# Moving the first query products between the passes of other units, and GpSimd's first sum behind VectorE's denominators, in a kernel of linear attention beside a dense SiLU layer

## The chip, the cores and the metric

The kernel runs on one core of one Trainium2 chip. The metric is device time in microseconds (us) of one execution; the median of three executions of the kernel before is 152.88 us, and they lie between 152.51 and 153.01 us. The profiled execution is one more, with a time of its own.

The engines are called PE (TensorE's matmuls), PEld (TensorE's weight loads, which run beside matmuls), DVE (VectorE), ACT (ScalarE), POOL (GpSimd) and SP (which issues transfers). PSUM has eight banks, numbered 0 to 7; a tile that is written by PE and read by DVE or ACT takes a pair of neighbouring banks, and the pair is named by its first bank.

## The reference, cut to what matters

```python
def _A_ref(x, wqkv, w_phi, wo):          # S=2048 rows, D=448, H=16 heads, Dh=28
    q, k, v = split(x @ wqkv)
    pq, pk = q @ w_phi, k @ w_phi        # per head
    phi_q = concat([softmax(pq), softmax(-pq)])
    phi_k = concat([softmax(pk), softmax(-pk)])
    kv = einsum("bhsf,bhsd->bhfd", phi_k, v)
    z  = einsum("bhsf->bhf", phi_k)
    num = einsum("bhqf,bhfd->bhqd", phi_q, kv)
    den = einsum("bhqf,bhf->bhq", phi_q, z)[..., None] + 1e-6
    return (num / den) @ wo              # heads laid side by side
def _B_ref(x, w1, w2):                   # w1: 448 x 1792, w2: 1792 x 448
    return silu(x @ w1) @ w2
xn = _layernorm(x)
return x + _A_ref(xn, ...) + _B_ref(xn, ...)
```

## The kernel before, in words

**Work and tiles.** The 2048 rows are 16 tiles of 128, taken as eight pairs (pair 0 to pair 7). After the layer norm each pair is transposed on PE (`xnT_tr` in `ln_tr`, L634: seven operations of two transposes each into a pair of banks, copied to `xnT` by DVE or ACT).

**Units and passes.** The first dense layer (`x @ w1`, then SiLU on ACT) is computed in units (`ffn1_chunk`, L743): two blocks of 128 hidden features for two pairs of rows, into one pair of banks. A contraction over 448 features is done in half arrays of 64 rows: an operation (`mms`, L445) issues two matmuls side by side, one on the upper and one on the lower 64 rows of the array, each into its own bank. `contract` (L476) makes a unit of two **passes**: a first of eight operations and a second of six, in which the two halves of the array change banks. Since the second pass adds to banks that the other half has written, its first operation waits on a semaphore until the last operation of the first pass has ended (`syncs`). Something put between the two passes on PE fills that wait. PE executes strictly in the order in which it was given its instructions.

**Order.** Every instruction is recorded in a list with its dependences, and a list scheduler (`schedule`, L218) puts the list of each engine in order. Where the order matters it is laid down by hand: `odeps` are edges within one engine that only order, `deps` are edges that become semaphore waits, and `chain` (L1012 to L1239) is the order of groups on PE from the key stage on.

**Stages.** (1) Layer norm, transposes and first units; (2) units for pairs 2 to 5, with the folding of `w_phi` into the weights of q and k; at its end the transposes of pairs 6 and 7 and the units of pairs 4 and 5 for blocks 8 to 11; (3) keys, values, exponentials (`k_macro`, `q_group`, `k_acc`); (4) the last units (blocks 12 and 13 for pairs 4, 5 and all 14 blocks for pairs 6, 7; called u[0] to u[7], each of two passes u[i][0], u[i][1]), the sum over the keys turned into the matrix `KVZ`, and between them the **query products** of pairs 0 and 1; (5) for each pair the second dense layer and `wo` (`out_pair`, L1186), with the query products of the pair after next.

**Query products and division.** `q_products` (L1082) makes for one tile of a pair eight operations of two matmuls of 60 columns; a pair's tile 0 goes to banks 2 and 3, its tile 1 to banks 4 and 5, for every pair. `uu[0]`, `uu[1]` are the two tiles of pair 0, `uu[2]`, `uu[3]` those of pair 1. `q_divide` (L1097) empties the banks on DVE, for pair 0 tile by tile: `R2` (L1108, reciprocals of the sums, from PSUM), `Dd` (L1110, one input from PSUM and one from SBUF), `den` (L1112, two inputs in SBUF), `rden` (L1115, one input in SBUF), `Gq` (L1116, `R2` times `rden`, two inputs in SBUF), `o12` (L1123, one input from PSUM and one from SBUF, which reads the banks out). The next products into these banks wait for that `o12`. Then POOL adds the two halves (`oadd`, L1145, both inputs in SBUF): for pair 0 first tile 0 (448 columns), then tile 1 in four pieces (8, 56, 336, 48 columns). The sums are transposed on PE (`oT_tr`), and the second layer's products read them.

Of the kernel before, what the change touches and what calls it, by code (L numbers as in the profile page):

```python
# [332 lines left out]
def bass_parallel_sum__linear_kernel_hedgehog__dense_activation_silu__prompt_kernel(  # L333
# [11 lines left out]
    NT, NPAIR = S // 128, S // 256  # L345
# [10 lines left out]
    with es:  # L356
        def sb(name, shape, dt):
            return es.enter_context(nc.sbuf_tensor(name, shape, dt))
# [48 lines left out]
        den = sb("den", [128, 2, 32], F32)  # L407
# [14 lines left out]
        P = _Prog()  # L422
# [8 lines left out]
        def d_dve(n, mode=1):  # L431
            return n * 1.042 / mode + 150.0
# [24 lines left out]
        def trs(parts, name):  # L457

            def fn(e):
                for dst, src, r in parts:  # L460
                    out = e.transpose(dst, src, ident[r, 64:128] if r == LO else ident[r, 0:64])  # L461
                return out
            P.op("pe", 32.0, fn, reads=[p[1] for p in parts] + [ident[:]], writes=[p[0] for p in parts],
                 table=64, name=name)

        def act(dst, src, func, name, table=None, scale=1.0):
            return P.op("act", d_act(_cols(src)), lambda e: e.activation(dst, src, func, scale=scale),  # L467
                        reads=[src], writes=[dst], table=table, name=name)

        def copy_dve(dst, src, name, dur):  # L470
            return P.op("dve", dur, lambda e: e.tensor_copy(dst, src), reads=[src], writes=[dst], name=name)  # L471
# [143 lines left out]
        def ln_stats(t):  # L615
            bnst(t)
            bnag(t)

        def ln_rstd(t0, t1):
            m2, r2 = mv[:, t0:t1, 1], rstd[:, t0:t1]  # L620
            v2, nh = ve[:, t0:t1], neghalf[:, t0:t1]
            P.op("dve", 160, lambda e: e.tensor_scalar(v2, m2, EPS_LN, None, ALU.add), reads=[m2], writes=[v2], name="ve")  # L622
            P.op("pool", 580, lambda e: e.tensor_tensor(r2, v2, nh, ALU.pow), reads=[v2, nh], writes=[r2], name="rstd")  # L623

        def ln_norm(p, t, eng="dve"):
            sl = p % NXN
            for c0, c1, o0 in (((0, D, 0),) if t % 2 == 0 else ((384, D, D), (0, 384, 512))):
                xn = xn_sb[:, sl, o0:o0 + c1 - c0]
                dur = 120 + (c1 - c0) * 0.6 if eng == "dve" else 120 + (c1 - c0) * 1.0
                P.op(eng, dur, lambda e, xn=xn, c0=c0, c1=c1: e.tensor_scalar(  # L630
                    xn, x_sb[:, t, c0:c1], mv[:, t, 0:1], rstd[:, t:t + 1], ALU.subtract, ALU.mult),
                    reads=[x_sb[:, t, c0:c1], mv[:, t, 0:1], rstd[:, t:t + 1]], writes=[xn], name="xn")

        def ln_tr(p, js, b0, eng):  # L634
            for i, j in enumerate(js):
                trs([(bank16[b0 + h][:, 64 * i:64 * i + 64], xn_sb[r, p % NXN, 128 * j:128 * j + 128], r)
                     for h, r in enumerate((UP, LO))], "xnT_tr")
            n = len(js)
            src = psum16[:, b0 * 1024:(b0 + 2) * 1024].rearrange("p (b c) -> p b c", b=2)[:, :, 0:64 * n].rearrange(
                "p b (j u) -> p b j u", u=64)  # L640
            dst = xnT[:, js[0]:js[-1] + 1, p, :].rearrange("p j (b u) -> p b j u", b=2)
            if eng == "act":
                act(dst, src, ACTF.Identity, "xnT_ev")
            else:
                copy_dve(dst, src, "xnT_ev", d_dve(128 * n, 2))
# [79 lines left out]
        def ln_pair(p, one_by_one=False):  # L725
            t0, t1 = 2 * p, 2 * p + 1
            for t in (t0, t1):
                ln_stats(t)
                if one_by_one:
                    ln_rstd(t, t + 1)  # L730
            if not one_by_one:
                ln_rstd(t0, t1 + 1)
            ln_norm(p, t0)
            ln_norm(p, t1)
            ln_tr(p, [0, 1, 2, 3, 4, 5, 6], {3: 4, NPAIR - 1: 2}.get(p, 6), "act" if p in LN_ACT else "dve")

        LN_ACT = (2,)
        silus = []
# [2 lines left out]
        units_done = []  # L741
# [100 lines left out]
        for p in range(2):  # L842
            for f0, f1, i0, i1 in ((0, 6, 0, 2), (0, 6, 2, 3), (6, 10, 0, 2), (10, FT, 0, 2)):
                if p == 1 and i0 == 0 and f0 < 10:
                    k = len(P.ops)
                    ln_pair(2 + f0 // 6, f0 > 0)
                    evp.append(P.ops[-1])
                    ln_late.append(P.ops[k:])
                    for o in P.ops[k:]:
                        if o.eng == "dve":  # L850
                            o.odeps.add(last1)
                passes.append(ffn1_single(p, f0, f1, i0, i1, next(banks_), f0 + p + i0 == 0))
                if p + f0 + i0 == 0:
                    k = len(P.ops)
                    evp.append(lnz_second(1))
                    for o in P.ops[k:]:
                        if o.eng == "dve":
                            o.odeps.add(ev0.id)
                    last1 = [o.id for o in P.ops if o.eng == "dve"][-1]
# [4 lines left out]
        turn = d2[:5] + d3[:6] + d2[5:] + d3[6:]  # L864
# [6 lines left out]
        for a, c in zip(order0, order0[1:]):  # L871
            for o in c:
                o.odeps.add(a[-1].id)
        k = len(P.ops)
        ln_pair(4)
        later4 = [o for o in P.ops[k:] if o.eng == "dve"]
        tr4 = [o for o in P.ops[k:] if o.name == "xnT_tr"]
        evp.append(P.ops[-1])
        unit_no[0] = 0
        ffn1_chunk(2, 2, 0, 4, (4, 0, 2))  # L880
        k = len(P.ops)
        ln_pair(5)
        later5 = [o for o in P.ops[k:] if o.eng == "dve"]
        for o in later4 + later5:
# [23 lines left out]
        for o in P.ops[k:]:  # L908
            if o.eng == "dve":
                o.odeps.add([a for a in later5 if a.name == "xn"][-1].id)  # L910

        def proj(p, W, b0, name):
            return contract([(lambda r, b: xnT[r, b, p, :], W,
                       [banks[b0 + par][:, 0:D] for par in range(2)], True, False)], D, True, True, name)
# [29 lines left out]
        def k_acc(p):  # L944

            sl, ops = p % NEK, []
            for t in range(2):
                first, last = p == 0 and t == 0, p == NPAIR - 1 and t == 1
                E3 = Ek[sl][:, t, :].rearrange("p (s c) -> p s c", s=2)
                for c in range(4):  # L950
                    parts = []
                    for i in range(4):
                        h = 4 * c + i
                        parts.append((banks[4][VW * i:VW * i + VW, 56 * c:56 * c + 56].rearrange("p (s f) -> p s f", s=2),
                                      vaug[sl][:, t, h, :], E3[:, :, h * DH:h * DH + DH], first and c == 0, last))
                    ops.append(mms(parts, "kv_mm", 50.0, 32))
            return ops
# [54 lines left out]
        chain = []  # L1012
# [22 lines left out]
        kv = k_acc(NPAIR - 3) + k_acc(NPAIR - 2) + k_acc(NPAIR - 1)  # L1035
# [38 lines left out]
        kv_tr = kv_transpose()  # L1074
# [20 lines left out]
        oadd_last = {}  # L1095
# [129 lines left out]
        u = units_done[k:]  # L1225
        uu = []
        for p in range(2):
            uu += marked(q_products, p)
            q_divide(p)
        uu = [uu[8 * i:8 * i + 8] for i in range(4)]  # L1230
        chain += [u[0][0], u[1][0], u[0][1], u[2][0], u[1][1], u[2][1], kv, u[3][0], kv_tr, u[3][1], u[4][0][:4], uu[0],
                  u[4][0][4:], uu[1], u[4][1], u[5][0], u[5][1], u[6][0], uu[2], u[6][1], u[7][0], uu[3], u[7][1]]
        for p in range(NPAIR - 1):
            out_pair(p)
        out_last(NPAIR - 1)
        chain = [c for c in chain + out_order if c]
# [20 lines left out]
        for e in ("pe", "act", "dve", "pool"):  # L1257
            cnt = 0
            for oid in order[e]:
                o = ops[oid]  # L1260
# [4 lines left out]
        for e in ENGINES:  # L1265
            for oid in order[e]:
                o = ops[oid]
# [88 lines left out]
```

## Time and profile before

| | |
|---|---|
| median of three executions | 152.88 us (152.51 to 153.01) |
| the profiled execution | 152.47 us |
| its span, first to last instruction | 150.8 us (1.67 us lie outside) |
| PE busy | 147.0 us, 2698 matmuls |
| DVE busy | 99.5 us |
| ACT busy | 73.0 us |
| POOL busy | 56.3 us |
| granted TensorE clock | 1.000 |

A line of the timeline gives the start, the time to the end of the last of a run of like instructions, the engine, the source line, the operation, the tiles, the count and, in brackets, the idle time ahead of it and what ended it. A matmul's shown duration includes its way through the array, so that neighbours overlap; the rate at which PE works is read from the starts. Units stand there as `psum<-xnT,w_sb`, query products as `psum<-KVZ,EqT`, the second dense layer as `psum<-w_sb,hT`, transposes of rows as `psum<-ident,xn_sb`. Two matmuls are one operation.

### The profile page before, as it was taken

The page shows a single profiled execution, that of the slowest core. Times are in us where ns is not written, and L with a number is a line of the kernel's source. Part 1 is how long each engine was busy: PE and PEld are TensorE (multiplying, and loading weights), DVE is VectorE, ACT ScalarE, POOL GpSimd, SP SyncE. Part 2 cuts the span into 40 slices and gives each one's busy share as a digit, 9 for nine tenths or more (in the row PEclk, how much of TensorE's full clock was granted, in tenths as well). Part 3 has the DMA queues.
Part 4 walks back from the last instruction along what each step waited for, and adds up shares of the span by engine and source line. Part 5 has one row for each costly group of instructions (what it writes and reads, how often), then busy time and mean ns, then how long its engine had stood idle before and what let it go on. Part 6 is the DMA issues. An engine that isn't in the chain of part 4 may idle for free.

```text
span 150.8 us, 5942 instructions
## 1 busy us (share of the span) xinstructions
PE 147.0 (98%) x2698; PEld 102.4 (68%) x2698; DVE 99.5 (66%) x189; ACT 73.0 (48%) x84; POOL 56.3 (37%) x85
## 2 busy tenths in 40 slices
PE   7999999999999999999999999999999999999992
PEld 6789988888844445446488885666666666665672
DVE  1989798965518999489693678748383939392203
ACT  3648865567699886888497555202020202022000
POOL 7135031020101788847993054370707070614000
DMA  4988374000004332253201000010101010101012
GB/s 119 347 257 262 99 218 130 5 4 4 4 0 122 126 122 67 55 151 49 36 12 16 4 0 4 4 61 4 61 4 61 7 61 4 61 0 65 0 65 61
DMA packets 9427, 10.30 MB, mean 68 GB/s; under 512 B 1626, under 2 KB 9018, under 8 KB 9402
## 3 DMA queue, kind: packets, MB, share of 16 engines
q1 hardware_dynamic: 8938, 9.65, 21.8%
q8 instruction: 21, 0.34, 0.9%
q10 hardware_dynamic: 464, 0.28, 0.6%
q14 instruction: 4, 0.03, 0.1%
HBM read 7.37 MB, written 1.84 MB: 61 GB/s over the span
## 4 chain that ended last, share of the span: by engine, by line
PE 98%; DVE 0%; issue 0%
PE psum L448 94%; PE psum L461 3%; DVE out_raw L1174 0%; PE psum L1059 0%
## 5 line engine op out<-in xcount | busy, mean ns | idle before, releaser
L448 PE MATMUL psum<-w_sb,hT 64*128 64x448 bf16 (+2 forms) x504 | 46.8, 328 | 0.0
L448 PE MATMUL psum<-xnT,w_sb 64*128 64x256 bf16 (+1 forms) x768 | 46.5, 268 | 0.1
L448 PEld LDWEIGHTS psum<-xnT,w_sb 64*128 64x128 bf16 x768 | 36.1, 94 | 4.2 <-PE psum L448 0.3
L467 ACT ACTIVATE hT<-psum 128x1024 bf16<-128x1024 f32 (+1 forms) x29 | 28.2, 993 | 13.7 <-PE psum L448 13.7
L448 PEld LDWEIGHTS psum<-w_sb,hT 64*128 64x128 bf16 x504 | 25.0, 94 | 14.3
L1145 POOL TENSOR_TENSOR xn_sb<-wraw 128x448 bf16<-128x448 f32 (+4 forms) x39 | 20.7, 562 | 36.2 <-DVE wraw L1123 31.6
L467 ACT ACTIVATE oT<-psum 128x896 bf16<-128x896 bf16 x8 | 7.3, 917 | 40.2 <-PE psum L461 40.2
L939 POOL TENSOR_TENSOR scr<-scr,Rk 128x1792 bf16<-128x1792 bf16 (+2 forms) x7 | 19.0, 2725 | 13.6 <-ACT scr L467 11.1
L1123 DVE TENSOR_TENSOR wraw<-psum,Gq 128x1792 f32<-128x1792 f32 (+1 forms) x10 | 16.4, 1650 | 0.8
L1174 DVE TENSOR_TENSOR out_raw<-psum,x_sb 128x896 bf16<-128x896 f32 (+2 forms) x9 | 8.8, 980 | 9.6 <-PE psum L448 9.4
L467 ACT ACTIVATE EqT<-psum 128x1024 bf16<-128x1024 f32 x14 | 13.6, 1021 | 3.1 <-PE psum L448 3.1
L1108 DVE RECIPROCAL R<-psum 128x64 f32<-128x64 f32 (+1 forms) x9 | 4.6, 511 | 15.1 <-PE psum L448 15.1
L448 PE MATMUL psum<-wv_sb,xnT 64*128 64x448 bf16 x112 | 14.2, 349 | 0.0
L448 PE MATMUL psum<-wo_sb,oT 64*128 64x448 bf16 (+2 forms) x126 | 13.7, 328 | 0.0
L448 PE MATMUL psum<-wqk_sb,xnT 64*128 64x448 bf16 x112 | 13.2, 349 | 0.0
L448 PE MATMUL psum<-xnT,wqk_sb 64*128 64x512 bf16 (+1 forms) x112 | 12.9, 378 | 0.0
L623 POOL TENSOR_TENSOR rstd<-ve,neghalf 128x2 f32<-128x2 f32 (+1 forms) x9 | 6.0, 666 | 17.7 <-DVE ve L622 17.7
L931 DVE TENSOR_REDUCE Sk<-scr 128x64 f32<-128x1792 bf16 (+1 forms) x7 | 12.2, 1737 | 0.0
L608 DVE BATCH_NORM_STATS2 st<-x_sb 128x6 f32<-128x448 bf16 x16 | 9.7, 612 | 3.4 <-DMA x_sb<-in_A_x_dram 3.4
L467 ACT ACTIVATE scr<-psum 128x896 bf16<-128x896 f32 x12 | 10.3, 913 | 2.9 <-PE psum L448 2.3
L471 DVE CAST scr<-psum 128x896 bf16<-128x896 f32 x6 | 6.5, 1081 | 6.4 <-PE psum L448 6.4
L448 PEld LDWEIGHTS psum<-wo_sb,oT 64*128 64x128 bf16 x126 | 6.6, 94 | 4.1 <-ACT oT L467 0.2
(78 smaller groups left out, 138.9 us busy)
## 6 DMA issues: line engine op xcount, KB each, us to landing
out_dram<-out_raw SPq DMA_DIRECT2D x7, 224.0 KB, 1.9
w_sb<-in_B_w_dram SPq DMA_DIRECT2D x3, 448.0 KB, 3.4
x_sb<-in_A_x_dram SPq DMA_DIRECT2D x2, 448.0 KB, 4.3
w_sb<-in_B_w_dram SPq DMA_DIRECT2D x2, 384.0 KB, 6.2
x_sb<-in_A_x_dram SPq DMA_DIRECT2D x3, 224.0 KB, 5.0
w_sb<-in_B_w_dram SPq DMA_DIRECT2D x3, 224.0 KB, 3.4
wraw<-in_A_wqkv_dram SPq DMA_DIRECT2D x1, 672.0 KB, 4.5
w_sb<-in_B_w_dram SPq DMA_DIRECT2D x1, 576.0 KB, 4.3
```

The costliest lines, as they stand in the source:

```text
L448: r = e.matmul(dst, lhsT, rhs, start=start, stop=stop, skip_group_check=True)
L461: out = e.transpose(dst, src, ident[r, 64:128] if r == LO else ident[r, 0:64])
L467: return P.op("act", d_act(_cols(src)), lambda e: e.activation(dst, src, func, scale=scale), reads=[src], writes=[dst], table=table, name= ...
L471: return P.op("dve", dur, lambda e: e.tensor_copy(dst, src), reads=[src], writes=[dst], name=name)
L608: P.op("dve", 600, lambda e: e.bn_stats(st6[:, t, :], x_sb[:, t, :]), reads=[x_sb[:, t, :]], writes=[st6[:, t, :]], name="bnst")
L623: P.op("pool", 580, lambda e: e.tensor_tensor(r2, v2, nh, ALU.pow), reads=[v2, nh], writes=[r2], name="rstd")
L931: P.op("dve", d_dve(896 * n), lambda e, S4=S4, E4=E4: e.tensor_reduce(S4, E4, AXL.X, ALU.add), reads=[E4], writes=[S3], name="Sk")
L939: lambda e, E5=E5, R5=R5: e.tensor_tensor(E5, E5, R5, ALU.mult),
L1108: P.op("dve", d_rec(32 * n), lambda e, R3=R3, U=U: e.reciprocal(R3, U[:, :, :, DH + 1]), reads=[U[:, :, :, DH + 1]], writes=[r2], name="R2")
L1123: P.op("dve", d_dve(896 * m), lambda e, dsto=dsto, Uj=Uj, Gj=Gj, m=m: e.tensor_tensor(dsto, Uj[:, :, :, 0:DH], Gj[:, :, :, None].broadcast ...
L1145: lambda e, dst=dst, a0=a0, a1=a1: e.tensor_tensor(dst, a0, a1, ALU.add),
L1174: P.op("dve", d_dve(2 * (c1 - c0)), lambda e: e.tensor_tensor(dst, ob, xs, ALU.add), reads=[ob, xs], writes=[dst], name="out_ev")
```

## The change

Three edits. First, the transposes of pair 6 go to banks 2 and 3 and those of pair 7 to banks 6 and 7 (before, the other way round), and the seven transposes of pair 7 are ordered between the two passes of the last unit of stage 2 (`units_done[-1]`). Before, the scheduler placed them: one operation ahead of the second pass of the unit before the last, two in the middle of that pass (with all seven of pair 6), and four between the passes of the last unit. In the changed kernel the scheduler puts the seven of pair 6 between the passes of the unit before the last. Second, POOL's first sum of pair 0 waits for the second `den` of DVE, that of pair 0's tile 1, besides its own inputs. Third, on PE the products `uu[0]` go between the passes of u[4] whole (before: in the middle of its first pass), and `uu[1]` between the passes of u[5] (before: between the passes of u[4]); u[5]'s two passes had stood next to each other.

```diff
-            ln_tr(p, [0, 1, 2, 3, 4, 5, 6], {3: 4, NPAIR - 1: 2}.get(p, 6), "act" if p in LN_ACT else "dve")
+            ln_tr(p, [0, 1, 2, 3, 4, 5, 6], {3: 4, NPAIR - 2: 2}.get(p, 6), "act" if p in LN_ACT else "dve")
...
+        turn = [units_done[-1][0], [o for o in P.ops if o.name == "xnT_tr"][-7:], units_done[-1][1]]
+        for x, y in zip(turn, turn[1:]):
+            for o in y:
+                o.odeps.add(x[-1].id)
...
-        chain += [u[0][0], u[1][0], u[0][1], u[2][0], u[1][1], u[2][1], kv, u[3][0], kv_tr, u[3][1], u[4][0][:4], uu[0],
-                  u[4][0][4:], uu[1], u[4][1], u[5][0], u[5][1], u[6][0], uu[2], u[6][1], u[7][0], uu[3], u[7][1]]
+        P.ops[oadd_last[0][0]].deps.add([o.id for o in P.ops if o.name == "den"][1])
+        chain += [u[0][0], u[1][0], u[0][1], u[2][0], u[1][1], u[2][1], kv, u[3][0], kv_tr, u[3][1], u[4][0], uu[0],
+                  u[4][1], u[5][0], uu[1], u[5][1], u[6][0], uu[2], u[6][1], u[7][0], uu[3], u[7][1]]
```

The instructions of DVE, ACT, POOL and SP are the same and stand in the same order; those of PE are the same, in the order told.

## The prediction

> **What bounds the kernel now.** I read the shares of busy time first, then the chain of waits, then stretches of the timeline around the edits.
>
> ```profile
> PE 147.0 (98%) x2698; PEld 102.4 (68%) x2698; DVE 99.5 (66%) x189; ACT 73.0 (48%) x84; POOL 56.3 (37%) x85
> ...
> PE 98%; DVE 0%; issue 0%
> ```
>
> PE is the bound and has nearly no idle time: a matmul taken off its way, or a wait put on it, reaches the end of the kernel whole, and nothing behind 92 us would take it up (the pairs of stage 5 follow each other at 7.28 us, by the starts of their transposes in the chain, 103.60, 110.88, 118.16 and so on). So the question is only how much waiting PE loses and gains. The stretch 82.0 to 84.5 us of PE, then all engines from 86.0 to 89.5:
>
> ```profile
> 82.18 1.26 PE L448 MATMUL psum<-xnT,w_sb 64*128 64x256 bf16 x20
> 83.27 0.56 PE L448 MATMUL psum<-KVZ,EqT 56*128 56x60 bf16 x16
> 83.66 0.62 PE L448 MATMUL psum<-xnT,w_sb 64*128 64x256 bf16 x8
> ```
>
> ```profile
> 85.77 2.04 PE L448 MATMUL psum<-xnT,w_sb 64*128 64x256 bf16 x30
> 86.10 1.42 PEld L448 LDWEIGHTS psum<-xnT,w_sb 64*128 64x128 bf16 x28 [0.35 <-PE psum L448]
> ...
> 86.44 1.13 POOL L1145 TENSOR_TENSOR xn_sb<-wraw 128x448 bf16<-128x448 f32 x1 [6.05 <-DVE wraw L1123]
> 86.66 0.19 DVE L1110 TENSOR_TENSOR Dd<-psum,R 128x32 f32<-128x32 f32 x1
> 86.88 0.72 DVE L1112 SCALAR_TENSOR_TENSOR den<-Dd 128x16 f32<-128x16 f32 x1
> ...
> 87.63 0.25 DVE L1115 RECIPROCAL rden<-den 128x16 f32<-128x16 f32 x1
> 87.65 0.39 PE L448 MATMUL psum<-KVZ,EqT 56*128 56x60 bf16 x16
> ...
> 87.92 0.19 DVE L1116 TENSOR_TENSOR Gq<-R,rden 128x32 f32<-128x32 f32 x1
> 88.25 1.09 DVE L1123 TENSOR_TENSOR wraw<-psum,Gq 128x896 f32<-128x896 f32 x1
> ...
> 89.39 0.19 PEld L448 LDWEIGHTS psum<-KVZ,EqT 56*128 56x128 bf16 x8
> 89.42 0.20 POOL L1145 TENSOR_TENSOR xn_sb<-wraw 128x8 bf16<-128x8 f32 x1 [1.85 <-DVE wraw L1123]
> 89.42 0.25 PE L448 MATMUL psum<-KVZ,EqT 56*128 56x60 bf16 x6
> ```
>
> Three things are to be seen. First, u[5]: the last operation of its first pass starts at 85.77, the second pass at 86.11 (the other 28 of the 30 are 14 operations up to 87.65, 0.11 each). An operation takes 0.11, so the wait between passes costs 0.34 - 0.11 = 0.23 us. Where products stand between passes (87.65 to 87.88, 0.23) nothing is lost. Second, `den` of tile 1 took 0.72 us, that of tile 0 0.18; it ended at 87.60, 0.03 behind POOL's sum (86.44 + 1.13 = 87.57). So it waited for the sum. `Dd`, with one SBUF input, ran at its usual 0.19 under the same sum. Third, `o12` of tile 1 ended at 88.25 + 1.09 = 89.34, and the weight load of uu[3], which waits for it, came 0.05 behind that, its matmul 0.08: the load is normally 0.1 ahead of its matmul, here 0.03. **uu[3] is thus already set by DVE, with no slack**: any delay of this `o12` is PE time.
>
> One more stretch shows the same rule at another operation, VectorE's part of `phik` (two SBUF inputs):
>
> ```profile
> 78.70 0.89 DVE L939 TENSOR_TENSOR scr<-scr,Rk 128x448 bf16<-128x448 bf16 x1
> ```
>
> POOL's own sum at that place ran from 77.41 to 79.11 and its next one 1.32 us instead of the 0.94 that its 448 columns would take by the sums of 896 and 1792 columns (1.70 and 3.21, so 1.69 ns a column and 0.18 fixed): each was held until the other had ended.
>
> **The change part by part.**
>
> *Third edit, order of the products.* uu[0] comes four operations later: 83.27 + 4 x 0.109 = 83.71. uu[1] fills u[5]'s wait. If no product had to wait for DVE, PE would gain the 0.23 of u[5] and 0.01 at the first operation behind the wait, and uu[3] would start at 89.42 - 0.24 = 89.18. The waits on seven transfers in uu[0] (0.39 instead of 0.23 long) stay.
>
> But DVE's chain starts with uu[0], so 0.44 later. `R2` of tile 0 starts at 83.93 + 0.44 = 84.37, its `o12` ends at 86.36 + 0.44 = 86.80 (before, it ran 85.27 to 86.36, and `R2` of tile 1 began at 86.28); uu[2] (at 87.41) waits for that and has time. `R2` of tile 1 follows at 86.72, `den` starts at 86.88 + 0.44 = 87.32.
>
> *Second edit, POOL behind `den`.* With POOL idle `den` takes 0.18 and ends at 87.50: 0.54 saved. But POOL then starts at 87.50 + 0.08 = 87.58 (0.08 from a DVE end to POOL's start, as at 86.36/86.44 and 89.34/89.42) and runs 1.13, to 88.71. `rden` (one SBUF input) runs 87.53 to 87.78: I take it as free, since the reciprocal `Rk` of one SBUF input took 0.35 under POOL's sum at 78.31 and as much in the median without. **`Gq`, 0.03 behind it at 87.82, has two inputs in SBUF like `den` and comes 0.24 behind POOL's start.** The trace has no `Gq` under a sum: its cost lies between 0.19 (not held) and the whole rest of the sum, 88.71 + 0.19 - 87.82 = 1.08. I take the row of `den`, nearly the same operation with the same kind of inputs: end 0.03 to 0.05 behind the sum, 88.75.
>
> The Trainium skill, page "SBUF — State Buffer", section "SBUF: two separate sides", says that VectorE and GpSimd hold a shared pair of ports as an exclusive lock for a whole instruction, whoever starts first, and that on VectorE's side an operation with two SBUF inputs takes part. The rows of `den` and `phik` agree, and by the page `Gq` is held as well, which no row here shows; a reading of the rows alone, in which only `den` is held, gives the first rival's time.
>
> Behind `Gq` an event of 0.13 comes before `o12` (88.11 to 88.25 now): 88.88, its end 89.97, uu[3] at 90.05 with the 0.08 above. That is 0.63 later than the 89.42 of before, 0.87 later than PE could take it. Queued behind uu[3] on PE is all the rest of the kernel. Behind the held `Gq` on DVE only `o12` and the next pair's chain, which follow uu[3] anyway. POOL's four small sums of tile 1 start 0.08 behind `o12` as now; pair 0's transposes (now at 91.69, the sums' end at 90.98) move with uu[3] and keep 0.6 of slack.
>
> *First edit, transposes of pairs 6 and 7.*
>
> ```profile
> 40.04 0.30 PE L461 MATMUL psum<-ident,xn_sb 64*128 64x64 bf16 x8
> 40.28 0.28 PE L448 MATMUL psum<-xnT,w_sb 64*128 64x256 bf16 x2
> ```
>
> Four transposes last 0.12 us (40.04 to 40.16) and leave 0.12 of the last unit's wait open. Seven fill 0.21, and the wait ends about 0.34 behind the start of the last operation: 0.11 + 0.21 leaves 0.02, a gain of 0.10. Against it: pair 6's transposes now go to banks 2 and 3, one operation (0.11) earlier than pair 7's first went there, and these banks are read by a SiLU until 38.54 (37.52 + 1.02 on ACT); pair 7's first came at 38.60, 0.06 behind it. So that gap of up to 0.11 opens there, half hidden in unevenness that goes (the whole stretch has 0.16 over its operations' own time). I take -0.04, between -0.10 and +0.07. The bank swap also frees v of pair 0 from the last copy, which ended 0.65 ahead of it: nothing.
>
> **Sum.** +0.63 - 0.04 = +0.59 us. The profiled execution took 152.47, below all three timed ones; so 153.06 on its own scale, and on the median's 152.88 + 0.59 = **153.5 us**, slower by 0.4%. About 0.3% (0.46 us) is what a measurement of this kernel can tell from no change.
>
> **Rivals.**
>
> 1. *`Gq` isn't held* (or it takes the ports ahead of POOL, whose first step may need them only later). For: no row shows it held, and POOL's start lies only 0.24 ahead. Against: `den` and `phik`. Then `Gq` ends at 88.01, `o12` runs 88.14 to 89.23, uu[3] starts at 89.31, 0.11 earlier than before: -0.11 - 0.04 = -0.15, **152.7 us**. It decides at the point where `Gq` starts to be held: if the sum still holds it 0.15 or less, the change isn't slower.
> 2. *All waits go*: `o12` ends by 89.10 and both fillings are whole: -0.24 - 0.10, **152.5 us**. For: PE alone. Against: the chain of DVE as it stands in 1 is 0.13 too late.
> 3. *POOL isn't moved behind `den`* in effect, so that `den` is held as now: sum 86.88 to 88.01, `den` to 88.04, `rden` and `Gq` to 88.55, `o12` 88.69 to 89.78, uu[3] at 89.86: +0.44 - 0.04, **153.3 us**. For: the wait stands on the same semaphore as its old one. Against: it is a later count of it.
> 4. *The early stretch loses too*: pair 6's transposes wait and the stage of the keys starts later, +0.1 to +0.3 on top: **153.7 us**. For: the SiLU ends just there. Against: behind it PE runs units, which need no ACT result of that moment.
>
> **How the numbers follow.** My forecast 0.74, rival 1 0.13, rival 2 0.03, rival 3 0.04, rival 4 0.06. The range reaches from rival 1's time less a spread of 0.1 to rival 4's plus 0.1, as the three timed executions lie up to 0.37 apart: 152.6 to 153.8. Slower by over 0.3% is over 153.34: most of the forecast (0.56 of its 0.74, since 0.13 us of spread takes the rest below) and rival 4: 0.62. Faster by over 0.3% is under 152.42: a part of rivals 1 and 2, 0.06. Within 0.3%: 0.32.
>
> **What would show it.** In the profile after, `den` of tile 1 should take 0.18, and the second of the `Gq` over 128x32 about 0.93 instead of 0.19, ending with POOL's sum of 448 columns; the weight load of uu[3] should show about 0.8 us of idle time put down to DVE's `o12`; the wait ahead of u[5]'s second pass should be gone. A `Gq` of 0.19 beside a running sum makes my forecast wrong by 0.74 us; a sum that starts more than 0.32 behind `den` does the same.

## The result, and the profile after

The changed kernel takes 153.14 us in the median of 22 executions (152.83 to 154.28), the kernel before 152.75 us (152.31 to 153.23) in as many beside it. The ratio is 1.003, with a 95% interval of 1.0020 to 1.0041: slower, by 0.31 to 0.63 us. The forecast was 153.5 us, +0.59. The profiled execution took 153.07 us, its span is 151.34 us against 150.75 before.

The page's busy shares and its chain of waits for the changed kernel:

```profile
PE 147.0 (97%) x2698; PEld 103.4 (68%) x2698; DVE 99.8 (66%) x189; ACT 73.0 (48%) x84; POOL 56.3 (37%) x85
...
PE 94%; DVE 4%; issue 0%; DVEq 0%
```

PE does the same 147.0 us of work in a longer span, and DVE, which had no share of the chain before, now has 4% of it. That share is the length of the chain's way through VectorE (84.34 to 89.96), beside which PE went on working; it isn't the loss. The timeline of the changed kernel from the transposes of `KVZ` on (its line numbers are 4 higher from the middle of the file, so `den` is L1116, `Gq` L1120, `o12` L1127) shows where:

```profile
82.02 0.41 PE L1063 MATMUL psum<-ident,scr 64*128 64x64 bf16 x16
82.26 1.69 PE L448 MATMUL psum<-xnT,w_sb 64*128 64x256 bf16 x28
83.79 0.39 PE L448 MATMUL psum<-KVZ,EqT 56*128 56x60 bf16 x16
84.02 1.70 PE L448 MATMUL psum<-xnT,w_sb 64*128 64x256 bf16 x28
```

```profile
87.29 0.17 DVE L1116 SCALAR_TENSOR_TENSOR den<-Dd 128x16 f32<-128x16 f32 x1
...
87.54 1.13 POOL L1149 TENSOR_TENSOR xn_sb<-wraw 128x448 bf16<-128x448 f32 x1 [7.15 <-DVE den L1116]
...
87.79 0.94 DVE L1120 TENSOR_TENSOR Gq<-R,rden 128x32 f32<-128x32 f32 x1
...
88.86 1.09 DVE L1127 TENSOR_TENSOR wraw<-psum,Gq 128x896 f32<-128x896 f32 x1
90.00 0.28 PEld L448 LDWEIGHTS psum<-KVZ,EqT 56*128 56x128 bf16 x16 [1.02 <-DVE wraw L1127]
90.01 0.40 PE L448 MATMUL psum<-KVZ,EqT 56*128 56x60 bf16 x16 [0.74 <-DVE wraw L1127]
```

`den` fell from 0.72 to 0.17, and `Gq` rose from 0.19 to 0.94: it ends at 88.73, some 0.05 behind POOL's sum (87.54 + 1.13 = 88.67). The wait has not gone, it has moved to the next operation with two SBUF inputs. uu[3] then stands at 90.01, and a matmul that had no visible idle time before it now has 0.74.

**A ruler.** The start of the profiled executions scatters, so I measure uu[3] from the start of the transposes of `KVZ` (L1059, in the changed kernel L1063), which the third edit leaves in place. In the kernel before they stand here:

```profile
81.94 0.41 PE L1059 MATMUL psum<-ident,scr 64*128 64x64 bf16 x16
```

Before: 89.42 - 81.94 = 7.48 us. Changed: 90.01 - 82.02 = 7.99. From uu[3] to the end of the span it is 61.32 to 61.35 us in all twelve profiles of this study, so what uu[3] loses, the kernel loses.

### The profile page after: what moved, and what is told of

Same layout as the page of the kernel before. It is cut to its first block, busy times and chain, and to the rows that moved or that the text cites. A ratio compares the mean times of both kernels' runs of the same rounds, so it can differ in the third digit from the quotient of the medians.

```text
span 151.3 us, 5942 instructions
## 1 busy us (share of the span) xinstructions
PE 147.0 (97%) x2698; PEld 103.4 (68%) x2698; DVE 99.8 (66%) x189; ACT 73.0 (48%) x84; POOL 56.3 (37%) x85
## 4 chain that ended last, share of the span: by engine, by line
PE 94%; DVE 4%; issue 0%; DVEq 0%
PE psum L448 90%; PE psum L461 3%; DVE wraw L1127 1%; DVE Gq L1120 1%; DVE R L1112 0%; DVE rden L1119 0%; DVE out_raw L1178 0%; DVE Dd L1114 0%; DVE den L1116 0%; PE psum L1063 0%; DVEq L1301 0%
## 5 line engine op out<-in xcount | busy, mean ns | idle before, releaser
L1127 DVE TENSOR_TENSOR wraw<-psum,Gq 128x1792 f32<-128x1792 f32 (+1 forms) x10 | 16.4, 1650 | 0.8
```

The costliest lines, as they stand in the source:

```text
L1127: P.op("dve", d_dve(896 * m), lambda e, dsto=dsto, Uj=Uj, Gj=Gj, m=m: e.tensor_tensor(dsto, Uj[:, :, :, 0:DH], Gj[:, :, :, None].broadcast ...
```

## The experiments

The theory: a VectorE operation with two SBUF inputs waits until a running GpSimd sum has ended; the new order makes VectorE's chain 0.3 to 0.4 us late, and the new wait of POOL puts the sum on `Gq`. The main rival: the later products alone cost the time. Every kernel is compared with the kernel before on the same chip.

**The changed kernel without the second edit.**

```diff
-        P.ops[oadd_last[0][0]].deps.add([o.id for o in P.ops if o.name == "den"][1])
```

> The changed kernel without its second edit: POOL's first sum starts as soon as o12 of pair 0's tile 0 has ended. Theory (an operation of VectorE with two SBUF inputs is held until a running GpSimd sum ends): the sum runs 86.84 to 87.98, den of tile 1 is held to 88.01 (0.72 instead of 0.17), Gq is free again (0.19), uu[3] starts at 89.80, against 90.01 in the changed kernel and 89.42 before: 0.2 us faster than changed, 0.4 slower than before. Rival (the time was lost by the later products alone, and Gq's 0.94 is beside the point): as slow as the changed kernel, 0.6 above before.

Its timeline:

```profile
87.04 0.72 DVE L1116 SCALAR_TENSOR_TENSOR den<-Dd 128x16 f32<-128x16 f32 x1
...
88.09 0.19 DVE L1120 TENSOR_TENSOR Gq<-R,rden 128x32 f32<-128x32 f32 x1
...
89.56 0.40 PE L448 MATMUL psum<-KVZ,EqT 56*128 56x60 bf16 x16 [0.55 <-DVE wraw L1127]
```

The hold is back at `den`. With its transposes at 81.77, uu[3] is at 7.79: 0.20 earlier than in the changed kernel, 0.31 later than before. Ratio to before 1.0016 (1.0002 to 1.0030). So the second edit costs 0.20 us on top of what the order costs, and the rival is right in part: without the second edit, with the hold back at `den`, the order is slower too.

**The kernel before with the second edit alone**, the line above added to it.

> The kernel before with the second edit alone: order of PE as before, POOL's first sum behind den of tile 1. Theory: den 0.18, the sum 87.14 to 88.27, Gq held from 87.38 to 88.32 (0.94), o12 ends at 89.55, uu[3] at 89.60 instead of 89.42: 0.2 us slower than before. Rival (the later products alone cost the time): as before, or 0.2 faster at o12 with nothing to show for it on PE.

```profile
87.61 0.94 DVE L1116 TENSOR_TENSOR Gq<-R,rden 128x32 f32<-128x32 f32 x1
...
89.83 0.28 PEld L448 LDWEIGHTS psum<-KVZ,EqT 56*128 56x128 bf16 x16 [0.23 <-DVE wraw L1123]
89.83 0.40 PE L448 MATMUL psum<-KVZ,EqT 56*128 56x60 bf16 x16
```

89.83 - 82.16 = 7.67, 0.19 later than before, as expected. The times, at 1.0014 (0.9997 to 1.0032), agree but don't exclude no change.

**The changed kernel with POOL behind `Gq`.**

```diff
-        P.ops[oadd_last[0][0]].deps.add([o.id for o in P.ops if o.name == "den"][1])
+        P.ops[oadd_last[0][0]].deps.add([o.id for o in P.ops if o.name == "Gq"][1])
```

> The changed kernel with POOL's first sum behind Gq of tile 1 instead of its den. Theory: neither den (0.17) nor Gq (0.19) is held, o12 with one SBUF input isn't held by the sum that runs beside it (1.09), it ends at 89.20, uu[3] starts at 89.26: 0.75 us faster than the changed kernel and 0.15 faster than before. Rival (later products alone): still 0.4 to 0.6 slower than before.

```profile
87.85 0.19 DVE L1120 TENSOR_TENSOR Gq<-R,rden 128x32 f32<-128x32 f32 x1
...
88.12 2.54 POOL L1149 TENSOR_TENSOR xn_sb<-wraw 128x448 bf16<-128x448 f32 x4 [7.58 <-DVE Gq L1120]
88.17 1.09 DVE L1127 TENSOR_TENSOR wraw<-psum,Gq 128x896 f32<-128x896 f32 x1
...
89.32 0.40 PE L448 MATMUL psum<-KVZ,EqT 56*128 56x60 bf16 x16
```

With its transposes of `KVZ` at 82.08, uu[3] is at 89.32 - 82.08 = 7.24, 0.75 earlier than in the changed kernel and 0.24 earlier than before. `o12`, with one input in SBUF, runs its 1.09 under the sum. Ratio to before 0.9972 (0.9959 to 0.9985): in these executions this version is faster than the kernel before, where the changed kernel, at 1.003, is slower. The later products alone, with no operation held, thus cost nothing, and the main rival is out.

**The old order with POOL behind `Gq`, and the run above once more beside it.**

> The kernel before, in its old order on PE, with POOL's first sum behind Gq of tile 1: VectorE is freed of both holds, nothing else changes. Theory (before, uu[3] stood at the point where PE and VectorE were due together, 5.71 + 1.77 = 7.48 us behind the transposes of KVZ): den 0.17, Gq 0.19, o12 ends 0.54 earlier, and uu[3] stays at 7.48, since PE isn't ready earlier: time as before. Rival (the hold alone was the cost, and POOL behind Gq alone brings what the run with the new order and POOL behind Gq brought): uu[3] earlier by 0.24, 0.2 to 0.3 per cent faster.

> The changed kernel with POOL's first sum behind Gq, once more, beside the old order on the same chip. In two of six profiled executions of this order the wait between u[4]'s passes lasted 0.57 instead of 0.33. Theory: Gq 0.19, uu[3] 7.24 behind the transposes of KVZ (7.32 with the long wait), 0.2 to 0.4 per cent faster than before. Rival (POOL behind Gq brings it, not the order): no faster than the old order with POOL behind Gq.

The old order:

```profile
87.66 0.19 DVE L1116 TENSOR_TENSOR Gq<-R,rden 128x32 f32<-128x32 f32 x1
...
89.69 0.39 PE L448 MATMUL psum<-KVZ,EqT 56*128 56x60 bf16 x16
```

Neither operation is held, `o12` ends 0.6 us ahead of uu[3], and uu[3] stays at 89.69 - 82.21 = 7.48; ratio 1.0007 (0.9995 to 1.0020). In the kernel before the hold of 0.54 us at `den` thus cost PE nothing. The new order beside it again has 7.24; its ratio, 0.9985 (0.9968 to 1.0002), lies nearer to 1 than the 0.9972 of the first time, and its interval just reaches past 1. Beside each other the two took 152.38 (new order) and 152.76 us (old order) in the median. So the gain needs both, the new order and a VectorE chain that the sum doesn't hold; its size is 0.24 us at uu[3], and between nothing and 0.4% in the times.

**`rden` in PSUM.** In the changed kernel, with POOL still behind `den`, `Gq` gets one of its inputs from PSUM:

```diff
                 dn, rd = (a[:, q, 16 * t0:16 * t1] for a in (den, rden))
+                if p == 0 and t0 == 1:
+                    rd = banks[UB + 2 * t0][:, 480:496]
```

> The changed kernel, with one thing different: rden of pair 0's tile 1 is written to 16 free columns of that tile's own PSUM bank, so that Gq reads one input from SBUF and one from PSUM. POOL's sum still starts behind den, ahead of Gq. Theory (a hold needs two SBUF inputs on VectorE): Gq takes 0.19 under the running sum, o12 is neither held, uu[3] starts about 7.24 us behind the transposes of KVZ (changed kernel 7.99, before 7.48): 0.75 faster than changed, 0.2 to 0.25 faster than before. Rival (Gq is late for another reason than its inputs, such as its place behind the sum's start): Gq 0.94, as the changed kernel.

```profile
88.03 1.13 POOL L1151 TENSOR_TENSOR xn_sb<-wraw 128x448 bf16<-128x448 f32 x1 [7.12 <-DVE den L1118]
...
88.28 0.19 DVE L1122 TENSOR_TENSOR Gq<-R,psum 128x32 f32<-128x32 f32 x1
```

The same operation, at the same place behind the start of the same sum, takes 0.19 instead of 0.94. So the hold goes with the second SBUF input, not with the place. uu[3] is at 89.81 - 82.50 = 7.31, ratio 0.9971 (0.9956 to 0.9986).

**The sum in four pieces.**

```diff
-            segs = [seg(0, 0, 0, 448), seg(1, 448, 384, 392), seg(1, 456, 392, 448), seg(1, 512, 0, 336), seg(1, 848, 336, 384)]
+            segs = ([seg(0, c, c, c + 112) for c in range(0, 448, 112)] if p == 0 else [seg(0, 0, 0, 448)]) + [seg(1, 448, 384, 392), seg(1, 456, 392, 448), seg(1, 512, 0, 336), seg(1, 848, 336, 384)]
...
+        for o in oadd_last[0][:4]:
+            P.ops[o].deps.add([o.id for o in P.ops if o.name == "den"][1])
```

> The changed kernel with POOL's first sum cut into four of 112 columns, all behind den. Theory (the hold lasts as long as the one instruction that has the ports): the first piece lasts 0.42 and ends about 0.18 behind Gq's start, so Gq takes 0.20 to 0.25, uu[3] starts 0.7 earlier than in the changed kernel. Rival (a waiting VectorE operation is passed by the pieces that are queued on POOL): Gq is held until the fourth piece ends, 1.2 us or more, uu[3] 0.3 or more later than in the changed kernel.

```profile
87.32 1.56 POOL L1149 TENSOR_TENSOR xn_sb<-wraw 128x112 bf16<-128x112 f32 x4 [7.09 <-DVE den L1116]
...
87.56 0.23 DVE L1120 TENSOR_TENSOR Gq<-R,rden 128x32 f32<-128x32 f32 x1
```

The first piece lasts 0.42, to 87.74, the second runs to 88.12; `Gq` ends at 87.79. It waits for the piece that runs, not for those queued behind it. Ratio 0.9975 (0.9957 to 0.9992), uu[3] at 7.32.

**The waits on landed transfers.** Two kernels take them earlier, by the first three lines below (and, in the second kernel only, the last two): the kernel before, and the changed kernel with POOL behind `Gq`.

```diff
+        dd = sorted({d for o in uu[0] for d in o.deps if P.ops[d].is_dma})
+        for o, d in zip(u[2][0], dd):
+            o.deps.add(d)
...
+        k = [o for o in P.ops if o.name == "kvT"][0]
+        k.deps.update(d for d in [o for o in P.ops if o.name == "o12"][1].deps if P.ops[d].is_dma)
```

> The kernel before with the seven waits on landed transfers in uu[0] taken one by one by operations of u[2]'s first pass. In the changed kernel uu[0] lasted 0.23 with the waits in their place, which I had expected to stay at 0.39. Theory (the 0.155 in uu[0] is the handling of seven waits that PE's sequencer reaches too late, behind half a pass, and in time behind a whole one): uu[0] lasts 0.23 here too, all behind it, VectorE's chain and uu[3] with it, comes 0.155 earlier: 0.15 us faster than before. Rival (it is uu[0]'s place behind half a pass, not the waits): 0.39 stays, as before.

> As the run with POOL behind Gq, and two sets of waits on transfers that landed long ago are taken earlier, so that they are not met where they cost: the seven ahead of the fourth operation of uu[0] go one by one to operations of u[2]'s first pass, the two ahead of o12 of tile 1 go to the kvT operation on VectorE. Theory (both gaps, 0.155 on PE inside uu[0] and 0.10 on VectorE ahead of o12, are the handling of waits): uu[0] lasts 0.23, o12 starts 0.03 behind Gq and ends at 88.95, uu[3] starts at 89.01: 0.4 us faster than before, 1.0 faster than changed. Rival (the gaps are something else, or move with the waits): as the run with POOL behind Gq, 0.15 faster than before.

The kernel before with early waits:

```profile
83.34 0.39 PE L448 MATMUL psum<-KVZ,EqT 56*128 56x60 bf16 x16
83.57 0.60 PE L448 MATMUL psum<-xnT,w_sb 64*128 64x256 bf16 x8
```

From its start to that of the next operation uu[0] lasts 0.23 (83.57 - 83.34) instead of 0.39 (83.66 - 83.27 before), and uu[3] comes to 89.34 - 82.01 = 7.33, 0.15 earlier, as expected. The times don't show it: 1.0000 (0.9983 to 1.0017), an interval wider than the 0.1% in question. In the other kernel uu[0] lasts 0.23, but so it does with the waits in place in the new order. `o12` starts some 0.03 behind `Gq` (87.91 + 0.19 = 88.10, then 88.14, both rounded) instead of 0.13, and uu[3] is at 89.28 - 82.14 = 7.14, 0.10 earlier than without, not the 0.25 I had expected, since 0.155 of it had been there already. Its ratio, 0.9978 (0.9966 to 0.9990), can't be told from 0.9972.

**The first edit alone**, in the kernel before, with one profiled execution:

> The kernel before with the first edit alone (banks of pairs 6 and 7 swapped, pair 7's transposes between the passes of the last unit). Theory: the first keys' products start 3.49 us behind the last folding products instead of 3.53, 0.04 earlier, with a gap of about 0.1 ahead of pair 6's transposes that ends with the SiLU on ACT; the rest as before, uu[3] about 7.48 behind the transposes of KVZ. Rival (the early stretch gains or loses what the changed kernel shows in all): a stretch more than 0.1 shorter or longer.

The first keys' products start 41.01 - 37.71 = 3.30 us behind the last folding products (before 40.95 - 37.61 = 3.34, each from the start of the last two folding matmuls). uu[3] is at 89.57 - 82.08 = 7.49. I had named these distances 3.49 and 3.53, from another starting point; the difference of 0.04 is as expected.

## Why the prediction was right, and where it was not

- **PE is the bound, and a delay of uu[3] reaches the end whole**: right; 61.32 to 61.35 us from uu[3] to the end in every profile. That uu[3] had no slack before is right too, but PE was due there at the same moment as VectorE: with `o12` 0.6 us earlier, in the old order with POOL behind `Gq`, it stays at 7.48. The idle time ahead of uu[3]'s weight load is put down to `o12`, as forecast; it is 1.02 us, where I had said about 0.8.
- **u[5]'s wait of 0.23 goes**: right. uu[1] runs from 85.56 to 85.79 in its place and the second pass follows at once.
- **`den` is freed and `Gq` held**: right in place and size. Forecast 0.93, measured 0.94; POOL started 0.08 behind `den`, as assumed. The runs with `rden` in PSUM and with the sum in four turned it from a likeness to `den` into a shown cause. The Trainium skill, page "SBUF — State Buffer", section "SBUF: two separate sides", states the exclusive hold for a whole instruction and names two SBUF inputs on VectorE among its conditions; these runs agree with both, 0.94 against 0.19 with one SBUF input, and 0.23 with a shorter instruction. My reading of the `phik` row, that each operation was held until the other had ended, was too strong: POOL's second sum there ended at 77.41 + 2.98 = 80.39, only 0.80 behind VectorE's end at 79.59, where I had worked out 0.94 for a whole sum of its size. `Gq` too ends 0.05 behind the sum and takes 0.19 alone, so not the whole of a held operation waits.
- **"The waits on seven transfers in uu[0] stay"**: this step was wrong. uu[0] fell from 0.39 to 0.23 us (83.79 to 84.02). VectorE's chain, which begins with `R2`, therefore started 0.55 behind uu[0]'s start (84.34 - 83.79) and not 0.66 (83.93 - 83.27). It was 0.33 later than before (84.34 - 82.02 = 2.32 behind the transposes of `KVZ`, against 83.93 - 81.94 = 1.99), not 0.44; and uu[3] started 0.06 behind `o12`, not 0.08. Together uu[3] came 0.51 later and not 0.63. Moving the waits in the old order gave the same 0.23, so there it was the waits that cost; in the new order they cost nothing in their old place (the last section shows why). The starts of `R2`, before and after:

```profile
83.93 0.36 DVE L1108 RECIPROCAL R<-psum 128x32 f32<-128x32 f32 x1 [1.05 <-PE psum L448]
...
84.34 0.36 DVE L1112 RECIPROCAL R<-psum 128x32 f32<-128x32 f32 x1 [1.37 <-PE psum L448]
```

- **The transposes bring 0.04**: right, 3.34 to 3.30, with the forecast gap ahead of pair 6's (15 matmuls of units stand where 17 ran before in the same time):

```profile
38.60 0.26 PEld L461 LDWEIGHTS psum<-ident,xn_sb 64*128 64x128 bf16 x14 [0.18 <-ACT hT L467]
```

- **The sum**: +0.51 - 0.04 = +0.47 us, in the middle of the measured 0.31 to 0.63. That the profiled spans differ by just the forecast 0.59 is a coincidence: another 0.11 lies between the first keys' products and the transposes of `KVZ` (40.99 before, 41.10 after), a stretch without an edit, which takes between 40.95 and 41.10 over the twelve profiles, and 0.01 ahead of the last folding products. The forecast time of 153.5 is high also because it started from 152.88, where the kernel before took 152.75 beside the changed one.
- **Rival 1** (`Gq` not held) is what the kernel with POOL behind `Gq` shows, 0.24 faster at uu[3]. I had put it at 0.11, for the same mis-sized uu[0].
- **Rival 2** (all waits go): 0.24 was what I took PE to be able to gain at uu[3]. It can gain more, since the 0.16 in uu[0] goes too: with earlier waits and POOL behind `Gq` uu[3] came 0.34 earlier (7.14). That POOL behind `Gq` alone gave just 0.24 is chance, for uu[3] still waits for `o12` there (88.17 + 1.09 = 89.26, then 89.32).
- **Rival 3** (POOL's wait without effect) was 0.19 below the forecast in my sum, and 0.20 below the changed kernel in the run without it.
- **Rival 4** (the early stretch loses too) didn't come: pair 6's transposes wait, and the keys' products start 0.04 earlier all the same.

## What to carry to other kernels

When a GpSimd operation is moved to free one VectorE operation of its hold, look for the next operation of that chain with two SBUF inputs: here the hold moved from `den` to `Gq`. Three ways out worked in this kernel: the sum behind the last operation of the chain with two SBUF inputs, one input of that operation in PSUM, or the sum cut in pieces. A hold that the bound engine doesn't wait for is no gain to be had: here 0.54 us of it cost nothing, until another edit made VectorE's chain late. When work on the bound engine is moved to fill a wait, follow the chain on the other engine that begins with it.

## What the runs showed of the hardware that I had not expected

Seven waits on transfers that had landed long before (between 67.6 and 72.1 us in the kernel before, where uu[0] starts at 83.27) cost some 0.16 us on PE among operations of 0.03 us each, and nothing when a whole pass stood ahead of uu[0] in place of half a pass. The packed traces, which hold PE's wait instructions too, show why. Six of the seven waits are in three instructions that PE's queue reaches only behind its wait for `KVZ`, whose copy on ACT ends at 83.03 before and at 83.12 after. The three start 0.16, 0.27 and 0.38 us behind that end before, and 0.16, 0.27 and 0.47 after. uu[0]'s first matmul starts 0.24 behind it before and 0.67 after. With half a pass the last of the three falls into uu[0]; with a whole pass all are over.

In two of the seven profiles of the new order (`rden` in PSUM, and the sum in four) the wait between u[4]'s passes lasted longer, 0.46 us from uu[0]'s start to the second pass instead of 0.23, with the same instructions on PE in the same order. From the run with `rden` in PSUM:

```profile
84.27 0.39 PE L448 MATMUL psum<-KVZ,EqT 56*128 56x60 bf16 x16
84.73 1.42 PEld L448 LDWEIGHTS psum<-xnT,w_sb 64*128 64x128 bf16 x28 [0.19 <-PE psum L448]
```

It costs these two runs 0.07 to 0.08 at uu[3] (7.31 and 7.32 against 7.24). Its cause is open.
